# Hash-masked attention and a mixture of experts: new gates and slots for GpSimd's subtractions, other slots for weight copies and scatters, other numbers of idle matmuls

## The chip, the cores and the metric

The kernel runs on one core of a Trainium2 chip. The metric is the time of one execution on the device in microseconds (us). The engines are named as in the profile: PE is TensorE (matmuls; PEld its weight loads), DVE is VectorE, ACT is ScalarE, POOL is GpSimd, SP issues most of attention's DMAs. TensorE's clock has two levels, 1.2 and 2.4 GHz, and the profile gives the granted clock as a share of full speed.

## The reference, cut to what matters

Attention comes first: 4 batches of 8 heads, 768 rows of 64, with a mask of equal hash buckets. Its output, 3072 tokens of 512, goes through a mixture of 8 experts, where a greedy order over all (token, expert) scores assigns at most 384 tokens to each expert.

```
logits = x @ w_gate
flat = logits.flatten()
order = np.argsort(-flat)
assigned = -np.ones(N, dtype=np.int64)
counts = np.zeros(E, dtype=np.int64)
for idx in order:
    tok, e = (int(idx) // E, int(idx) % E)
    if assigned[tok] >= 0 or counts[e] >= cap:
        continue
    assigned[tok] = e
    counts[e] += 1
out = np.zeros((N, D), dtype=np.float32)
for e in range(E):
    mask = assigned == e
    h = np.maximum(x[mask] @ w1[e], 0.0)
    out[mask] = h @ w2[e]
```

N is 3072, D 512, E 8, cap 384, and w1[e] is 512 x 1024.

## The kernel before, in words

The program has two parts in an order written out by hand: each engine runs its instructions as the code lists them. Attention ends near 428 us; the expert part, class Moe, follows, and only that part is touched.

**Phases.** The greedy assignment is done in eight phases. In each phase the expert that fills up first is found ("closed"): DVE takes the best expert left for every token, then a threshold is searched digit by digit in six levels. A level is a comparison on DVE (zcmp), a count on PE (L472 for the first level and all of phase 0, L479 later), a few small DVE steps on the counts (L481 to L563), and a new running value zd (L565, in SBUF, read by the next comparison). After the sixth level come the closing steps: L574 and L575 on PE, L577 to L585 on DVE (L580 makes zwg, L582 asg, L584 and L585 the pair zSTb), then L601 and L602 on PE, which rank the members. Then ohp and Rr on DVE, the collect L611 on PE, and the list of the 384 tokens (zidx). Phase 0 runs alone, between attention and the first expert.

**Blocks and slots.** `Moe.run` lays the experts out in eight blocks of 68 slots (NS). Block k computes the expert of phase k. A slot is a few matmuls: slots 0 to 31 are layer 1 (eight groups f=0 to 7 of four slots, three matmuls each, into two PSUM buffers in turn), slots 32 to 67 layer 2 (three groups c of twelve slots, two matmuls each). Phase k+1 runs inside block k: the lists E1 (phase 1, in block 0), E2 (phase 2) and EV (phases 3 to 6) give the slot at which each step of the phase is put into the order, counted from the start of block k (a negative one lies in the block before it). `XS` and `XS1` give the slots of the next expert's transposes (L709), 57 or 61 and on.

**Both halves of a number.** Weights and activations are split into a rounded part and the rest, and the products of the parts are summed. ACT rounds a quarter of a layer's weights (wh, L691; slots W1 and W11 for layer 1, W2 for layer 2), and POOL subtracts (wl, L701, two instructions per quarter, 16 per expert). After each f ACT writes hh (L737) and DVE writes hl (L738), which frees the PSUM buffer.

**Hands.** The subtractions wait in a list (`s.pend`). `s.hand(n)` puts n of them into POOL's order, behind a copy of one element (ztick, L700) from a tile named by `s.gate`, so that POOL starts only when DVE has written that tile: zd in a level, zsatl after the sixth, zcum and zcc later. HS gives n for each step. A subtraction that no hand took goes out at a slot of its own (L803). On POOL's order stand also the DMAs that gather the tokens (L674), load the next expert's weights (L682) and scatter the outputs (L756, slots by SC).

**Idle matmuls.** `s.warm` puts matmuls of 128 columns on PE that nothing reads (L505). KW holds their numbers for eight places in phase 0 and before the first expert.

Of the kernel before, what the change touches and what calls it, by code (L numbers as in the profile page):

```python
# [8 lines left out]
F32 = mybir.dt.float32  # L9
F32R = mybir.dt.float32r  # L10
F16 = mybir.dt.float16
BF = mybir.dt.bfloat16
I32 = mybir.dt.int32
AF = mybir.ActivationFunctionType
ALU = mybir.AluOpType
# [5 lines left out]
 E0=[3, 5],  # L21
 E1=[3, 4],
 X=[2, 2, 5],
# [12 lines left out]
 OPS='b0 i3 i2 t0 b1 w5 r0 r2 w4 s0 w4 C1 r1 t1 c1 s1 B0 c0 D0 w2 w1 s4 w5 s2 s3 r3 v2 w5 v0 l0 l1 C0 m0 s5 w3 s6 r5 w2 l3 e0 e1 d0 u0 u1 s7 v1 l2 w0 m1 e2 | s8 | x0 | w0 | x1 s9 | r4 s10 | | | s11 m2 v3 f0 | x3 | | x2 | m3 | | | | | |')  # L36
PAT,E0,E1,DW,LEAD=(AP[k] for k in ('PAT','E0','E1','DW','LEAD'))
NB=dict(S=2,T=3,V=1)
HK=385
EMPTY=60000.0  # L40
def attention(tc, nc, ctx, qT, kT, vv, proj, wg, x_dram, L, jp, identf, B, late=None, after=None):
# [183 lines left out]
    def lo(h,kc,eng):  # L225
        p,l=PT[h,kc]
        eng.tensor_tensor(l,p,p.bitcast(BF)[:,1::2],op=ALU.subtract)  # L227
# [93 lines left out]
    def run(n):  # L321
        for f,a in at.get(n,[]): f(*a)
# [5 lines left out]
    for t in range(6*NH+LAG+6):  # L328
        h,s=divmod(t,6)
        first=(t-LAG)%6==5  # L330
        if first: av(t)
        if t<6*NH and t not in early: ST(h,s,0)
        for x in S_at.get(t,[]): S_pass(*x)
        run(2*t)
        if h<NH: ST(h,s,1)
        if t>=1 and (t-1)//6<NH:
            hh,ss=divmod(t-1,6)
            lo(hh,ss,V if ss in (E0 if hh<1 else E1 if hh<2 else PAT[hh%2]) or t==6*NH else G_)
        run(2*t+1)
        if not first: av(t)  # L340
# [5 lines left out]
SH=[25,20,15,10,5,0]  # L346
LOW=[1,1,1,1,1,0]
NT=[128,32,32,32,32,32]
E1=[-12,-4,-3,2,6,7,8,14,20,27,33,36,39,46]
E2=[-9,-8,-6,1,8,15,20,23,27,38]  # L350
EV=[-15,-14,-9,-3,5,12,20,25,29,37]
WL=[4,46]
W1=[45,50,57,63]
W11=[54,55,62,66]
HS=[0,2,2,2,2,2,2,1,1,0]
HB=46
BY=[-1,8,36]
W2=[3,6,10,16]
XS=[57,57,60,63]
XS1=[61,61,64,65]  # L360
KW=[1,0,4,0,2,19,7,1]
SC=15
class Moe:
    def __init__(s, tc, nc, ctx, N):
        s.tc,s.nc,s.N=tc,nc,N
# [67 lines left out]
    def t(s,shape,dt,name,**k): return s.sp.tile(shape,dt,name=name,**k)  # L433
# [73 lines left out]
    def phase(s,ph):  # L507

        nc,NC=s.nc,s.NC; V=nc.vector; T=nc.tensor; G_=nc.gpsimd
        last=ph==7; first=ph==0  # L510
        t=s.z
# [5 lines left out]
        if not last:  # L517
            P=s.Z
            D,E,mxu=P["D"],P["E"],P["mxu"]; d=E[:,0]
            CMP=[P["cmp"][l and 1+l%2] for l in range(6)]  # L520
            if not first:
                for i,f in enumerate(s.best(P,0,NC)):
                    if ph==1 and i==4: yield
                    f()
                s.gate=E[0:1,0,0:1]
                for c0,c1_ in ((0,12),(12,NC)) if ph==1 else ((0,NC),):
                    if ph==1: yield
                    s.compare(CMP[0],0,d,c0,c1_)
            tot=0
            for l,w in enumerate(WID):  # L530
# [3 lines left out]
                if l==0 or first:  # L534
# [3 lines left out]
                    if first:  # L538
                        if l==0: wp=s.wps(); s.warm(KW[7],wp)
                        s.warm(KW[0],wp)  # L540
                    for a,b in ((l+1,l+2),) if first else ((1,6),):
# [9 lines left out]
                if l==0 or first:  # L551
# [4 lines left out]
                    T.matmul(n,s.us[l][0:J],hit[0:J],start=True,stop=True)  # L556
                    if first: s.warm(KW[1],wp)
                else:
# [16 lines left out]
            T.matmul(pe[:,0:8],s.tiny[0:32],sat[0:32],start=False,stop=True)  # L575
            if first: s.warm(KW[2],wp)
            V.reduce_max(nn,pe[:,0:8],axis=AX.X)  # L577
# [23 lines left out]
        T.matmul(pp[:,0:2*NC],s.ntri,STb,start=True,stop=False)  # L601
        T.matmul(pp[:,0:2*NC],s.ones,cum,start=False,stop=True)  # L602
        if first: wp=s.psO.tile([128,512],F32,name="po"); s.warm(KW[3],wp)
        pm=t([128,NC],F32,"pm"); md=t([128,NC],BF,"md"); Gt=t([128,4,NC],F32,"Gt"); junk=t([128,1],F32,"junk")
        mi=t([128,NC],I32,"mi")
        ohp=s.t([128,NC//2,128,2],BF,"ohp",bufs=1); Rr=t([128,2,2,3,NC],BF,"Rr"); acc=t([128,NC],F32,"acc")
        def members(c0,c1):
# [2 lines left out]
        def collect(c0,c1):  # L610
            for g in range(c0,c1): T.matmul(pi[:,0:12],ohp[:,g//2,:,g%2],Rr[:,:,:,:,g],start=g==0,stop=g==NC-1)  # L611
# [2 lines left out]

        V.tensor_scalar(mi,pm.bitcast(I32),0x4583F800,None,op0=ALU.bitwise_and)
        V.tensor_tensor(Gt,pm[:,None,:].to_broadcast([128,4,NC]),s.th,op=ALU.is_ge)
        V.tensor_scalar(md,mi.bitcast(F32),-4096.0,0.0,op0=ALU.add,op1=ALU.add,accum_out=junk)
        def left():

            V.tensor_tensor(A1,wg[:,None,:].to_broadcast([128,8,NC]),s.wt[:,:,None].to_broadcast([128,8,NC]),op=ALU.is_equal)  # L620
            with nc.allow_low_precision("counts up to 24"):
                V.reduce_sum(cc,A1,axis=AX.X)
            s.gate=cc[0:1,0:1]
# [12 lines left out]
        def rr():  # L636
            for i in range(2): V.tensor_tensor(Rr[:,i],Gt[:,None,i:i+3].to_broadcast([128,2,3,NC]),s.gp[:,i,:,None,:].to_broadcast([128,2,3,NC]),op=ALU.mult)
        if first:
            pi=ps()
            for i,b in enumerate(blocks):  # L640
                members(*b)
                if not i: rr()
                collect(*b); s.warm(KW[4],wp)
        else:
# [131 lines left out]
    def run(s):  # L776
        V=s.nc.vector; ch=s.ch; at={}; NS=68
        def add(n,f,*a): at.setdefault(n,[]).append((f,a))
        def end(p):
            s.gather(p)  # L780
            if p<7: next(ch[p+1])
        def step(p,n):
            next(ch[p],None); s.hand(n)
        for p in range(1,8):
            b=NS*(p-1)
            ev=[b+e for e in (E1 if p==1 else E2 if p==2 else EV)]
            dec=ev[-3] if p<7 else ev[-2]-2
            hs=[0]*(len(ev)-10)+HS
            if p==1: hs[3]=2
            if p==7: ev=ev[-2:]; hs=[0,0]  # L790
            for e,n in zip(ev,hs): add(e,step,p,n)
            add(ev[-1],end,p)
            if p>1: add(b-NS+HB,s.hand,2)
            add(max(dec,b+WL[0]),s.wload,p,0); add(max(ev[-1],b+WL[1]),s.wload,p,1)
            for q in range(4):
                add(b+(W11 if p==1 else W1)[q],s.wsplit,p,0,q,None,b+NS+BY[0]+BY[1]*q if p<6 else 0)
                add(b+(XS1 if p==1 else XS)[q],s.xsplit,p,q)
        for k in range(8):
            for q in range(4): add(NS*k+W2[q],s.wsplit,k,1,q,None,NS*k+BY[2] if k<6 else 0)
            for q in range(3): add(NS*k+44+12*q+SC,s.scatter)  # L800
        for n in range(-NS,NS*8):
            for f,a in at.get(n,()): f(*a)
            while s.pend and s.pend[0][0]<=n: s.nc.gpsimd.tensor_tensor(*s.pend.pop(0)[1],op=ALU.subtract)  # L803
            if n<0: continue
            k,h=divmod(n,NS)
            if h<32: s.layer1(k,h//4,h%4)
            else: s.layer2(k,(h-32)//12,(h-32)%12)
        while s.late: s.scatter()
# [52 lines left out]
```

## Time and profile before

| | |
|---|---|
| median of 3 runs | 789.22 us (785.79, 789.22, 791.88) |
| profiled execution | 785.28 us, of which span 783.5 us |
| PE busy | 718.4 us (92%), 7765 matmuls |
| DVE busy | 561.4 us (72%) |
| POOL busy | 550.8 us (70%) |
| ACT busy | 406.0 us (52%) |
| POOL's subtractions L701 | 90, 113.9 us, 1280 ns each |

The span is the time from the first to the last instruction on the core; the rest of the profiled execution's time lies around it. Busy shares are averages over attention and experts, which have different limits. In a row of a timeline stand the start in us, the duration, the engine, the line, the operation, output and inputs, and in brackets how long the engine stood idle before it and what ended that.

### The profile page before, as it was taken

The numbers are of one execution on the slowest core, as the hardware profiler recorded it, in microseconds if no ns is written. First come the engines' busy times: TensorE is split into PE (matmuls) and PEld (weight loads), VectorE is DVE, ScalarE is ACT, GpSimd is POOL, SyncE is SP. The second block draws the span as 40 slices with busy tenths as digits, with TensorE's granted clock in tenths as the row PEclk, the third lists the DMA queues.
The fourth block names the chain that finished last, engine by engine and source line by source line (L and its number), as shares of the span: only waits on it lengthen the run. The fifth ranks groups of instructions, "written<-read, shape, count | busy, mean of one in ns | idle before, by whom it ended". The sixth has DMA issues, their size and how long they took to land. (4 is left out here: it accounts for less than half of the span.)

```text
span 783.5 us, 19133 instructions
## 1 busy us (share of the span) xinstructions
PE 718.4 (92%) x7765; PEld 547.7 (70%) x7765; DVE 561.4 (72%) x1321; ACT 406.0 (52%) x790; POOL 550.8 (70%) x479
## 2 busy tenths in 40 slices
PE   8998999998999998999798579989999999999995
PEld 2566676666666675666566368877888787889894
DVE  5878978778677785988774768888887878753120
ACT  6776686576776766755555042524343334334430
POOL 7696788695785966856565167678878787878761
PEclk9999999999999998999999569999999999999998
DMA  6637734437254272340001160716171717162601
GB/s 182 192 89 194 169 119 126 103 115 167 70 121 109 84 175 51 85 104 22 22 2 41 33 225 1 269 47 236 41 255 41 256 42 255 41 222 92 251 27 41
DMA packets 38320, 92.40 MB, mean 118 GB/s; under 512 B 4452, under 2 KB 28888, under 8 KB 36184
## 3 DMA queue, kind: packets, MB, share of 16 engines
q1 hardware_dynamic: 31416, 45.03, 22.4%
q0 software_dynamic: 6816, 46.15, 16.6%
q8 instruction: 61, 1.00, 0.6%
q14 instruction: 27, 0.22, 0.1%
HBM read 59.53 MB, written 12.58 MB: 92 GB/s over the span
## 5 line engine op out<-in xcount | busy, mean ns | idle before, releaser
L227 POOL TENSOR_TENSOR lo<-pt 128x768 f16<-128x768 f32 x143 | 235.2, 1655 | 102.8 <-ACT pt L224 92.9
L224 ACT ACTIVATE pt<-pst 128x384 f32<-128x384 f32 x384 | 182.9, 491 | 94.0 <-PE pst L223 79.9
L200 DVE TENSOR_REDUCE m<-pss 128x1 f16<-128x770 f32 x192 | 182.6, 956 | 56.4 <-PE pss L198 55.4
L222 PE MATMUL pst<-qa,ka 128*128 128x384 f16 x384 | 128.2, 334 | 9.9 <-ACT pt L224 6.7
L223 PE MATMUL pst<-qb,kb 128*128 128x384 f16 x384 | 127.0, 331 | 0.0
L239 PE MATMUL psv<-vh,lo 128*128 128x65 f16 x1152 | 122.6, 195 | 0.0
L237 PE MATMUL psv<-vh,pt 128*128 128x65 f16 x1152 | 122.6, 196 | 0.0
L238 PE MATMUL psv<-vl,pt 128*128 128x64 f16 x1152 | 122.5, 194 | 0.0
L237 PEld LDWEIGHTS <-pt 128*128 128x128 bf16 x1152 | 107.8, 99 | 13.9 <-issue 4.4
L701 POOL TENSOR_TENSOR wl<-wf,wh 128x512 fp32r<-128x512 f32 x90 | 113.9, 1280 | 0.0
L238 PEld LDWEIGHTS <-pt 128*128 128x128 bf16 x1152 | 106.7, 99 | 10.1 <-issue 0.8
L198 PE MATMUL pss<-ka,qa 96*128 96x385 f16 x384 | 96.9, 334 | 12.9 <-ACT qa L208 7.8
L239 PEld LDWEIGHTS <-lo 128*128 128x128 f16 x1152 | 106.8, 98 | 0.0
L691 ACT CAST wh<-wf 128x1024 fp32r<-128x1024 f32 x64 | 66.4, 1048 | 47.3 <-DMA wf<-in_w_dram,zwidx 47.3
L737 ACT ACTIVATE hh<-ph 128x384 fp32r<-128x384 f32 x64 | 31.4, 491 | 86.7 <-PE ph L735 86.7
L198 PEld LDWEIGHTS <-qa 96*128 96x128 f16 x384 | 37.9, 99 | 45.2 <-issue 23.0
L738 DVE SCALAR_TENSOR_TENSOR hl<-ph,hh 128x384 fp32r<-128x384 f32 x64 | 35.2, 554 | 44.1 <-ACT hh L737 43.6
L735 PE MATMUL ph<-xh,wh 128*128 128x384 f32 x256 | 60.5, 349 | 2.0 <-DVE hl L738 1.2
L227 DVE TENSOR_TENSOR lo<-pt 128x768 f16<-128x768 f32 x49 | 58.6, 1195 | 2.0 <-ACT pt L224 1.9
L735 PE MATMUL ph<-xl,wh 128*128 128x384 f32 x256 | 56.8, 340 | 0.0
L735 PE MATMUL ph<-xh,wl 128*128 128x384 f32 x256 | 56.1, 339 | 0.0
L223 PEld LDWEIGHTS <-kb 128*128 128x128 f16 x384 | 38.2, 99 | 23.7 <-issue 13.5
(258 smaller groups left out, 1399.9 us busy)
## 6 DMA issues: line engine op xcount, KB each, us to landing
vp<-in_vv_dram SPq DMA_DIRECT2D x8, 768.0 KB
x_dram<-X SPq DMA_DIRECT2D x16, 384.0 KB
qp<-in_qT_dram SPq DMA_DIRECT2D x7, 768.0 KB
kp<-in_kT_dram SPq DMA_DIRECT2D x7, 768.0 KB
qa<-qh SPq DMA_DIRECT2D x14, 192.0 KB
ka<-kh SPq DMA_DIRECT2D x14, 192.0 KB
qb<-qh SPq DMA_DIRECT2D x14, 192.0 KB
kb<-kh SPq DMA_DIRECT2D x14, 192.0 KB
```

Of the source, the lines that this page charges most:

```text
L198: T.matmul(ps[:,hf,0:HK],QA[u][0:96,j,qc*128:qc*128+128],KA[u][0:96,j,hf*HK:hf*HK+HK],start=True,stop=True)
L200: V.tensor_reduce(M6[h][:,qc:qc+1],ps[:,:,0:HK],axis=AX.XY,op=ALU.max,negate=True)
L222: T.matmul(ps[:,0:384],KA[u][:,j,kr],QA[u][:,j,r],start=True,stop=False)
L223: T.matmul(ps[:,0:384],KB[u][:,j,kr],QB[u][:,j,r],start=False,stop=True)
L224: A.activation(PT[h,kc][0][:,r],ps[:,0:384],AF.Exp,scale=0.125)
L227: eng.tensor_tensor(l,p,p.bitcast(BF)[:,1::2],op=ALU.subtract)
L237: T.matmul(av[:,c,:],ph[:,r],VH[u][:,j,kc,:],start=(kc==0 and c==0),stop=False,skip_group_check=True)
L238: T.matmul(av[:,c,0:64],ph[:,r],VL[u][:,j,kc,:],start=False,stop=False,skip_group_check=True)
L239: T.matmul(av[:,c,:],l[:,r],VH[u][:,j,kc,:],start=False,stop=False,skip_group_check=True)
L691: s.nc.scalar.copy(h[:,r],f[:,r])
L701: for _ in range(n): s.nc.gpsimd.tensor_tensor(*s.pend.pop(0)[1],op=ALU.subtract)
L735: T.matmul(p[:,0:384],a[:,o:o+128],b[:,d],start=n==0,stop=n==11)
```

## The change

Steps of phase 1 from the count on come three to five slots later in block 0 (E1). HS has other numbers: hands of three behind the first, second, fourth and fifth level's zd, of two behind the third, none behind the sixth level and the closing steps, two behind zcc. The additional hand of two at slot 46 (HB) is gone. The gate at a phase's start is the tile OH, written after E. ACT's rounded weights come at earlier slots: W1 from 45, 50, 57, 63 to 45, 48, 52, 57, and W2 from 3, 6, 10, 16 to 2, 4, 7, 11. Scatters are listed 7 slots after their group's end instead of 15 (SC). KW goes from [1,0,4,0,2,19,7,1] to [1,4,5,10,2,30,5,2]: four idle matmuls more at each level of phase 0 (second number), one and ten more at its closing (third, fourth), eleven more after its list (sixth), two fewer after each of three groups of transposes (seventh), one more at the first count (eighth). The step md no longer writes an accumulator. As two lines fall away, lines of after have numbers one or two lower.

```diff
-E1=[-12,-4,-3,2,6,7,8,14,20,27,33,36,39,46]
+E1=[-12,-4,-3,2,11,12,13,19,25,31,37,40,43,49]
-HS=[0,2,2,2,2,2,2,1,1,0]
-HB=46
+HS=[0,3,3,2,3,3,0,0,2,0]
...
-                s.gate=E[0:1,0,0:1]
+                s.gate=P["OH"][0:1,0,0:1]
...
-        V.tensor_scalar(md,mi.bitcast(F32),-4096.0,0.0,op0=ALU.add,op1=ALU.add,accum_out=junk)
+        V.tensor_scalar(md,mi.bitcast(F32),-4096.0,None,op0=ALU.add)
...
-            if p>1: add(b-NS+HB,s.hand,2)
```

POOL's order in block 3, from the scatter of the block before's last group to the closing of phase 4, before:

```order
L756 DMA out_dram<-o,zidx 3072x512
L700 CAST ztick<-zsatl 1x1
L701 TENSOR_TENSOR wl_10560<-wf_10353,wh_10559 128x512 x2
L700 CAST ztick<-zcum 1x1
L701 TENSOR_TENSOR wl_10560<-wf_10353,wh_10559 128x512
L682 DMA wf_10751<-in_w_dram,zwidx 128x4096
L700 CAST ztick<-zcc 1x1
```

After, from the same scatter:

```order
L755 DMA out_dram<-o,zidx 3072x512
L699 CAST ztick<-zd_10674 1x1
L700 TENSOR_TENSOR wl_10576<-wf_10374,wh_10575 128x512 x3
L681 DMA wf_10765<-in_w_dram,zwidx 128x4096
L699 CAST ztick<-zcc 1x1
L700 TENSOR_TENSOR wl_10576<-wf_10374,wh_10575 128x512 x2
L673 DMA xg<-x_dram,zidx 128x512 x3
```

The hand of two behind zsatl and the one subtraction behind zcum, which stood between the last levels and the load of the next weights, are gone; a hand of three now stands behind the fifth level's zd, after the scatter, and two subtractions instead of one behind zcc, ahead of the gather (xg).

DVE's order at the start of block 0, from the first comparison of phase 1 (zcmp_377), before:

```order
L461 TENSOR_TENSOR zcmp_377<-zE,tb_92 128x1536 x2
L738 SCALAR_TENSOR_TENSOR hl<-ph,hh 128x384
L456 TENSOR_SCALAR zD<-zkey 128x24 x5
L553 TENSOR_SCALAR zsat,zhit<-psa 128x8
L565 SCALAR_TENSOR_TENSOR zd_8898<-zE,psa 128x24
L461 TENSOR_TENSOR zcmp_379<-zd_8898,tb_93 128x768
```

After, from the same comparison:

```order
L460 TENSOR_TENSOR zcmp_377<-zE,tb_92 128x1536 x2
L737 SCALAR_TENSOR_TENSOR hl<-ph,hh 128x384 x2
L455 TENSOR_SCALAR zD<-zkey 128x24 x5
L552 TENSOR_SCALAR zsat,zhit<-psa 128x8
L737 SCALAR_TENSOR_TENSOR hl<-ph,hh 128x384
L564 SCALAR_TENSOR_TENSOR zd_8956<-zE,psa 128x24
L460 TENSOR_TENSOR zcmp_379<-zd_8956,tb_93 128x768
```

The digits (zD), the check of the first count (zsat) and the first level's zd stood behind hl of f=0 alone; now hl of f=0 and f=1 stand ahead of the digits, and hl of f=2 ahead of zd.

## Rows read from the trace of the kernel before

**Rows 1.** Busy time by stretches: start and end, length, then busy time (and count) of PE, PEld, DVE, ACT, POOL, the granted clock, the DMA share and GB/s.

```profile
460.00:480.00 20.00, 16.16 (x114) 14.63 (x113) 16.46 (x61) 8.08 (x17) 12.64 (x13) 0.83 0.30 106
...
550.00:600.00 50.00, 48.55 (x332) 42.90 (x333) 40.36 (x154) 20.42 (x35) 40.19 (x42) 1.00 0.35 124
```

**Rows 2.** The list of PE's waits from 466 to 784 us: what waited for what, us in total, times, longest.

```profile
PE psa L601 <- DVE zwidx L666: 5.4, 4, 2.0
PE psa L601 <- DVE zSTb L585: 1.2, 1, 1.2
```

**Rows 3.** Timelines of POOL, DVE and PE at the closing of phases 4 (block 3) and 2, and L580's durations over the whole run in ns (shortest/median/longest).

```profile
601.43 2.53 POOL L701 TENSOR_TENSOR wl<-wf,wh 128x512 fp32r<-128x512 f32 x2
...
601.90 2.10 DVE L580 SCALAR_TENSOR_TENSOR zwg<-zd,znn,zmxu 128x24 f32<-128x24 bf16 x1
...
L580 DVE SCALAR_TENSOR_TENSOR zwg<-zd,znn,zmxu x7: 232/2042/2098, 444.2 to 681.7; 128x24 f32<-128x24 bf16 x7
...
519.96 3.17 DVE L582 TENSOR_TENSOR asg<-asg,zwg 128x24 f32<-128x24 f32 x1
...
604.72 0.20 PE L601 MATMUL psa<-zSTb,ntri 128*128 128x48 bf16 x1 [1.18 <-DVE zSTb L585]
```

**Rows 4.** Timelines of POOL, DVE and PE in block 3, levels of phase 4.

```profile
584.94 2.54 POOL L701 TENSOR_TENSOR wl<-wf,wh 128x512 fp32r<-128x512 f32 x2
...
588.03 0.24 DVE L565 SCALAR_TENSOR_TENSOR zd<-zd,zn,zE 128x24 bf16<-128x24 bf16 x1
...
588.31 0.56 DVE L461 TENSOR_TENSOR zcmp<-zd,tb 128x768 bf16<-128x768 bf16 x1
...
589.49 0.32 PE L479 MATMUL psa<-zOH,zcmp 128*128 128x32 bf16 x6
...
593.39 0.32 PE L479 MATMUL psa<-zOH,zcmp 128*128 128x32 bf16 x6
```

**Rows 5.** Timelines of PE, POOL, DVE and ACT at the start of block 0.

```profile
458.87 0.96 PE L735 MATMUL ph<-xh,wh 128*128 128x384 f32 x4 [0.28 <-ACT xh L722]
...
461.61 2.49 POOL L701 TENSOR_TENSOR wl<-wf,wh 128x512 fp32r<-128x512 f32 x2
...
461.51 4.27 DVE L461 TENSOR_TENSOR zcmp<-zE,tb 128x1536 bf16<-128x1536 bf16 x2
...
464.97 0.48 PE L472 MATMUL psa<-zOH,zcmp 128*128 128x8 bf16 x12 [2.71 <-DVE zcmp L461]
...
465.50 1.04 ACT L691 CAST wh<-wf 128x1024 fp32r<-128x1024 f32 x1 [4.03 <-DMA wf<-in_w_dram,zwidx]
...
466.97 0.56 DVE L738 SCALAR_TENSOR_TENSOR hl<-ph,hh 128x384 fp32r<-128x384 f32 x1 [1.19 <-ACT hh L737]
...
469.43 1.63 PE L735 MATMUL ph<-xh,wh 128*128 128x384 f32 x4
```

**Rows 6.** Timelines of POOL, PE and DVE in block 0, the third and fourth level of phase 1.

```profile
472.87 0.50 POOL L700 CAST ztick<-zd 1x1 f32<-1x1 bf16 x1 [1.16 <-DVE zd L565]
...
473.57 0.32 PE L479 MATMUL psa<-zOH,zcmp 128*128 128x32 bf16 x6
...
473.93 0.15 DVE L481 TENSOR_TENSOR znt<-rem,psa 32x8 f32<-32x8 f32 x1
...
475.99 0.24 DVE L565 SCALAR_TENSOR_TENSOR zd<-zd,zn,zE 128x24 bf16<-128x24 bf16 x1
...
476.27 0.56 DVE L461 TENSOR_TENSOR zcmp<-zd,tb 128x768 bf16<-128x768 bf16 x1
...
477.47 0.96 PE L735 MATMUL ph<-xh,wh 128*128 128x384 f32 x4 [0.20 <-DVE hl L738]
```

**Rows 7.** Timelines of PE, DVE and POOL at the end of phase 1, and the time from issue to landing of the gathers (xg) over the whole run.

```profile
487.92 0.20 PE L601 MATMUL psa<-zSTb,ntri 128*128 128x48 bf16 x1
...
490.69 0.52 DVE L637 TENSOR_TENSOR zRr<-zGt,gp 128x144 bf16<-128x144 f32 x2
...
491.39 0.81 PE L611 MATMUL psa<-zRr,ohp 128*128 128x12 bf16 x24
...
495.39 1.11 POOL L674 DMA_INDIRECT xg<-x_dram,zidx  x1 [0.30 <-issue]
...
DMA to landing us min/median/max: 3.4/4.3/5.4
...
499.87 0.82 PE L709 MATMUL px<-identf,xg 128*128 128x128 f32 x6
```

**Rows 8.** Phase 0: three stretches (columns as in rows 1), and the timeline of PE for a count of 24 in phase 0 and one in phase 4.

```profile
434.00:436.00 2.00, 1.37 (x27) 1.02 (x27) 1.37 (x9) 0.00 (x0) 0.00 (x0) 0.50 0.01 4
...
454.00:456.00 2.00, 1.82 (x12) 1.76 (x13) 0.99 (x7) 1.15 (x2) 1.66 (x2) 0.50 0.68 184
...
457.00:458.00 1.00, 1.00 (x11) 1.00 (x9) 0.45 (x1) 0.52 (x1) 1.00 (x2) 0.62 0.91 344
...
434.46 0.96 PE L472 MATMUL pst<-zOH,zcmp 128*32 128x8 bf16 x24 [0.60 <-DVE zcmp L461]
...
577.25 0.76 PE L472 MATMUL psa<-zOH,zcmp 128*128 128x8 bf16 x24
```

**Rows 9.** Timelines of ACT and PE at the start of block 6.

```profile
708.06 1.06 ACT L691 CAST wh<-wf 128x1024 fp32r<-128x1024 f32 x1 [2.21 <-DMA wf<-in_w_dram,zwidx]
...
710.15 0.96 PE L735 MATMUL ph<-xh,wh 128*128 128x384 f32 x4 [0.77 <-DVE hl L738]
```

More of the change, by code (lines that the diff above doesn't have):

```diff
@@ L352 @@
 WL=[4,46]
-W1=[45,50,57,63]
+W1=[45,48,52,57]
 W11=[54,55,62,66]
-HS=[0,2,2,2,2,2,2,1,1,0]
-HB=46
+HS=[0,3,3,2,3,3,0,0,2,0]
 BY=[-1,8,36]
-W2=[3,6,10,16]
+W2=[2,4,7,11]
 XS=[57,57,60,63]
 XS1=[61,61,64,65]
-KW=[1,0,4,0,2,19,7,1]
-SC=15
+KW=[1,4,5,10,2,30,5,2]
+SC=7
 class Moe:
@@ L603, in phase @@
         if first: wp=s.psO.tile([128,512],F32,name="po"); s.warm(KW[3],wp)
-        pm=t([128,NC],F32,"pm"); md=t([128,NC],BF,"md"); Gt=t([128,4,NC],F32,"Gt"); junk=t([128,1],F32,"junk")
+        pm=t([128,NC],F32,"pm"); md=t([128,NC],BF,"md"); Gt=t([128,4,NC],F32,"Gt")
         mi=t([128,NC],I32,"mi")
```

## The prediction

> **What bounds the kernel now.** I read the chain of work that ended last first: it holds only the last scatter and its DMA, so the end hangs on TensorE (PE), which feeds the last tiles. The table of stretches comes next [rows 1]: from 550 to 600 us PE is busy 48.6 of 50 us at the full granted clock, from 460 to 480 us only 16.2 of 20 at 0.83. So in the expert part time can only be won where PE stands still or runs at 1.2 GHz. The list of PE's waits [rows 2] names one place: the matmul L601 waits five times, 6.6 us in all, for VectorE's (DVE) closing steps. The timelines say why [rows 3]: the step L580 takes 0.23 us when free and 2.10 us at 601.90, and ends when a pair of GpSimd (POOL) subtractions ends (601.43 + 2.53 = 603.96). At 519.96 L582 takes 3.17 us in the same way. So a DVE step on two SBUF inputs stands until POOL has finished all subtractions that it was handed, not only the running one. One subtraction is 1.27 us.
>
> **Part 1: no hand at the two last steps (HS).** The hands after the sixth level and at the closing are now empty, so L580 and L582 run free there and L601 gets its input about 1.9 us sooner than it did; the wait of 1.18 us at 604.72 [rows 3] and its like, up to 2.0 us [rows 2], should go. The 16 subtractions stay; they move into hands of three behind levels 1, 2, 4 and 5. A hand begins when the compare ends, since POOL's small copy waits for the same step. In blocks 2 to 5 a hand of three from 584.94 [rows 4] would end at 588.74. The level's step L565 (zd), due at 588.03, is held 0.7 us; the compare then ends near 589.4, and its reader on PE stands at 589.49. So the slack is used up and the slip is 0.1 to 0.2 us. The same holds a level later (a hand of two that begins after a scatter, reader at 593.39), and at the next. Behind each compare lies the step hl that frees a PSUM buffer for PE, which slips with it. I take 0.5 us of slip per block against a wait of (6.6 - 2.0) / 4 = 1.15: 0.65 us x 4 = **-2.6 us**, between -4.6 (no slip) and +2 (1.65 us of slip). In block 1, whose slots lie closer (E2), the slips eat all of the 2.0 us: **0**, between -2 and +1.5.
>
> **Part 2: phase 1 at later slots (E1), in block 0.** Before, PE stands 2.71 us at 464.97, because the compare is held by POOL's pair (461.61 to 464.10, compare from 461.51 for 4.27) [rows 5]. After, the count stands five slots later, and the pair waits for OH, a step later than E. That removes this wait, but what is late next stands beside it: ScalarE copies the first quarter of layer 2's weights at 465.50, when its DMA lands, and only then makes hh of f=0; hl of f=0 ends at 466.97 + 0.56 = 467.5. PE has two buffers for layer 1, so f=2 can't start before 467.6, with count or without. A slot of layer 1 is (3.90 - 0.17) / 7 = 0.53 us by the readers at 589.49 and 593.39 [rows 4]; eight slots from 458.87 end at 463.1. PE then idles 4.5 us where it idled 2.71 and worked through the count, the rest of f=1 and the first level. Before, f=2 starts at 469.43, so 1.8 us is won there, and a whole level of phase 1 is owed.
>
> How the level chain runs after: f=2 at half clock (four matmuls 1.63 us at 469.43 [rows 5]) and the count of 24 (0.96 us at half clock [rows 8]) end near 472.5. hh and hl of f=2 now stand ahead of L565 on DVE (0.5 + 0.56), then L565 and the compare: reader of level 1 near 474.6. A level takes 3.4 us undisturbed [rows 6]: reader to first step 0.36 (473.57 to 473.93), to L565 2.06, L565 and compare 0.84 (475.99 to 476.83), and 0.1 to the next reader. Six slots are 3.2 us, so this alone costs 0.2 a level. With a hand of three from the end of the compare (3.8 us), L565 is held 1.3 us: the reader of level 2 comes at 479.2, that of level 3 at 484.8. The latter holds a second price: hl of f=4 stands behind level 2's compare on DVE, and f=6 can't start without its buffer (the row at 477.47 shows that wait, 0.20 us, where one more slot lay between reader and f). Hands of two follow, so levels 4 and 5 come at 488.2 and 491.4, L601 at 494.5. From L601 to the end of Rr are 3.29 us (487.92 to 490.69 + 0.52) [rows 7], so the collect L611 comes at 497.8, against 491.39: 6.4 us later. The third gather is issued 4.0 us after L611 (495.39) and lands 4.3 us later by the median, 506.1; the transposes L709 keep their slot 61, and stood at 499.87. **+6.2 us** at that point, between +2 (the hands hold nothing and only f=2's late start and the buffer wait count) and +8. The new order of ScalarE's copies (W2) has no price of its own here: the copy that waits for the DMA stands before hh of f=0 in both.
>
> At this place a rule speaks for another sum. In the rows a held step waits for the whole hand [rows 3]. The Trainium skill, "SBUF — State Buffer", section "SBUF: two separate sides", says that the shared pair is an exclusive lock held for one whole instruction, and that a GpSimd op or a DVE op on two SBUF inputs blocks the other. By that rule DVE could slip in between two subtractions, and the time would be 789 (the first rival below); the rows at 601.90 and 519.96 disagree with that part.
>
> **Part 3: idle matmuls (KW).** Before the first expert, PE waits for DVE at each level. Four more idle matmuls per level, 0.43 us at half clock (an estimate: 128 columns at 1.2 GHz each), lie in the 0.60 us that the next count waits for its compare: nothing on the path. At the levels PE is busy 1.37 of 2 us and the granted clock is 0.50, that is 1.2 GHz; in 454 to 456 it was busy 1.82 of 2, and the clock rose to 2.4 GHz at 457 to 458 [rows 8]. So with more idle matmuls a rise may come earlier. If it does, a count of 24 takes 0.76 instead of 0.96. I take three levels: **-0.6 us**, between +0.3 (the eleven more after the closing, 1.2 us, reach past the landing of the first gather) and -1.5 (all levels, and the collects). Two fewer idle matmuls after each group of transposes would start PE 0.4 us sooner, but f=2 waits for the DMA anyway: 0.
>
> **Part 4: the rest.** Layer 1's weights are copied at earlier slots and loaded sooner, as the load isn't queued behind a subtraction: in block 6 ScalarE waits 2.21 us for a DMA ahead of hh, and PE 0.77 for it [rows 9]. An earlier load removes that: **-0.8**, between -0.8 and 0. Scatters move forward eight slots on POOL; hands of three stand behind them, 1 us each, and that is in the walk above. The plain subtraction in place of one with an accumulator (md) saves one short read per phase, and no subtraction of POOL runs beside it any more: 0. The dropped hand at slot 46 frees L565 of the first level, where PE had slack. Nothing at the tail changes.
>
> **The sum**, against the profiled execution (785.28 us, span 783.5): -0.6 + 6.2 + 0 - 2.6 - 0.8 = +2.2, so 787.5. The three other runs lie at 785.79, 789.22 and 791.88, and the four average 788.0; I put the same +2.2 on that: **790 us**. One per cent, 7.9 us, is about what a measurement of this kernel tells from no change.
>
> **Rivals.**
> - *DVE slips in between two subtractions.* Then L565 at 477.0 waits only for the second one, which ends there, and part 2 costs 5.0: -1.2, some 789. The two held steps speak against it. This is the rule of the Trainium skill's "SBUF — State Buffer" named above. Chance 0.12.
> - *L601 still waits.* The hand of three behind level 5 begins late, after a scatter, runs to 602.6, and holds L580 (601.90) again. Then part 1 is lost: +2.6, 792.5. Against it: 0.6 us of cover at L601. Chance 0.12.
> - *Faster: block 0 keeps up.* If the later count meets a compare that is ready and the levels aren't held, PE loses neither the 2.71 us at the count nor the waits at L601: -6.6 - 0.8 - 0.6 - 2.7 = -10.7, some 777. For it: these are PE's largest waits. Against it: the landing at 465.5 and the 3.8 us of a hand of three. Chance 0.11.
> - *Slower: the hands of three set the pace in blocks 1 to 5.* Slack between compare and reader is 589.49 - 588.87 = 0.6 us [rows 4]. A hold of 0.7 uses it up; if hands begin 0.6 us later than I put them (a tick takes 0.50 us [rows 6], and it may wait for the compare first), each of three levels in five blocks loses 0.6: +9, and part 1's gain goes: 790 + 9 + 2.6 = 801.6. It decides where the hold passes 0.7. Chance 0.11.
>
> **How the numbers follow.** The forecast, part 2's loss paid back by two thirds by parts 1, 3 and 4, gets 0.54. With the first two rivals, 0.78 lie within 1% of 789.2; 0.11 are faster, 0.11 slower. The range reaches to the near edges of both outer cases, and takes in the bounds of parts 1 to 3 and the spread of the runs: 780 to 798.
>
> **What would show it.** Right: PE waits from 463 to 467.6 for hl; level readers of block 0 stand 4.5 us or more apart; L565 takes up to 1.5 us there and 0.3 to 0.9 in blocks 2 to 5; L580 takes 0.23; L601's wait is gone; blocks 2 to 5 are each some 0.65 us shorter; the first L709 stands near 505.5. Wrong: L565 stays at 0.24 us beside hands of three, f=2 starts before 467, or L601 waits on.

## The result, and the profile of the changed kernel

The changed kernel takes 788.86 us (median of 20 runs, 784.69 to 797.49), the kernel before beside it 784.24 (20 runs, 778.45 to 791.88). The ratio is 1.0059, interval 1.0038 to 1.0081: some 4.6 us slower, 3.0 to 6.4. The forecast of 790 us and "within 1%" came out. The sum behind it did not hold as well: one term that it put at nothing was worth about 4 us, and of the gains set against the loss in block 0 two did not show and one came at most in part.

The profiled execution of the changed kernel took 787.92 us, its span is 785.8. Spans alone don't compare: attention ended 6.6 us sooner in this profile. In all profiles of this study the count of phase 0's second level stands anywhere from 424.2 to 437.7 us, with no code of attention altered. So I read the **expert part**, from that count to the end: 783.5 - 434.46 = 349.0 us before, 785.8 - 427.86 = 357.9 after. It spares the comparison attention's spread, but a single profile of it still differs by up to 5 us from what the ratios say (here +8.9 against +4.6). Part of that is the one profile of before: against it ten of the thirteen later profiles read 0.8 to 4.8 us too slow, and three up to 1.7 too fast. The largest of these gaps is that of the kernel with the old scatter slots, whose profile is the longest of its 11 runs. I trust the part for places, and for sums only where the ratio agrees.

Times of the changed kernel in the first block carry the shift: add 6.6 us to compare them with rows of before. Its lines have numbers 1 lower (L601 is L600), 2 lower at the end.

PE's waits from 459 to 786 us (what waited for what, us in total, times, longest). The waits of L601 [rows 2] are gone; two that were small in the kernel before (1.2 and 0.6 us there, as L735 and L556) stand in their place, L734 for hl and L555 for L552:

```profile
PE ph L734 <- DVE hl L737: 6.7, 8, 3.5
PE psa L555 <- DVE zsat L552: 5.7, 4, 1.5
PE psa L478 <- DVE zcmp L460: 2.5, 3, 1.4
```

Stretches (columns as in rows 1), the first and second 6.6 us earlier than those of [rows 1]; in the third, inside the first, PE has been at half clock throughout:

```profile
453.40:473.40 20.00, 15.75 (x91) 14.04 (x89) 13.11 (x37) 7.44 (x14) 10.87 (x11) 0.66 0.29 105
543.40:593.40 50.00, 48.19 (x332) 41.48 (x331) 40.01 (x152) 21.00 (x38) 39.79 (x39) 1.00 0.39 137
460.00:473.00 13.00, 12.12 (x65) 10.95 (x65) 6.68 (x26) 4.47 (x11) 6.23 (x7) 0.50 0.00 1
```

Block 0, timelines of ACT, PE, DVE and POOL, the answer to [rows 5 to 7]. PE stands 3.53 us for hl (2.71 for the compare before), then the level readers come at 467.17, 473.22, 477.75, 481.14 and 484.46, and L708 at 500.74:

```profile
458.08 1.04 ACT L690 CAST wh<-wf 128x1024 fp32r<-128x1024 f32 x1 [3.48 <-DMA wf<-in_w_dram,zwidx]
460.16 0.69 PE L734 MATMUL ph<-xh,wh 128*128 128x384 f32 x1 [3.53 <-DVE hl L737]
467.11 3.72 POOL L700 TENSOR_TENSOR wl<-wf,wh 128x512 fp32r<-128x512 f32 x3
469.61 1.27 DVE L564 SCALAR_TENSOR_TENSOR zd<-zd,zn,zE 128x24 bf16<-128x24 bf16 x1
473.22 0.32 PE L478 MATMUL psa<-zOH,zcmp 128*128 128x32 bf16 x6
487.83 0.20 PE L600 MATMUL psa<-zSTb,ntri 128*128 128x48 bf16 x1
491.16 0.50 PE L610 MATMUL psa<-zRr,ohp 128*128 128x12 bf16 x13 [0.23 <-DVE zRr L636]
500.74 1.48 PE L708 MATMUL px<-identf,xg 128*128 128x128 f32 x6
```

Blocks 2 to 5: the closing step L579 (durations in ns, whole run) against [rows 3], the level step L564 from 470 to 700 us against the 0.24 us of [rows 4], and the first level of phase 4 at block 3's head, POOL, DVE and PE:

```profile
L579 DVE SCALAR_TENSOR_TENSOR zwg<-zd,znn,zmxu x7: 232/490/528, 437.6 to 685.5; 128x24 f32<-128x24 bf16 x7
...
L564 DVE SCALAR_TENSOR_TENSOR zd<-zd,zn,zE x24: 243/610/1269, 469.6 to 679.9; 128x24 bf16<-128x24 bf16 x24
...
578.98 0.17 PE L472 MATMUL psa<-nrem,moneh 128*128 128x8 f16 x1
579.33 1.00 POOL L755 DMA_INDIRECT out_dram<-o,zidx  x1 [0.30 <-ACT zE L545]
580.99 0.17 DVE L552 TENSOR_SCALAR_CACHE_REDUCE zsat<-psa 128x8 bf16<-128x8 f32 x1 [2.37 <-PE po L746]
581.22 0.16 PE L555 MATMUL psa<-zhit,us 128*128 128x1 bf16 x1 [1.51 <-DVE zsat L552]
```

L579 falls from 2.04 to 0.49 us in the median (0.23 when free), so the closings run nearly as foreseen. But L564 takes 0.61 us where it took 0.24, and at the head of the block L552 starts 1.84 us after the count that it reads has ended (578.98 + 0.17), 0.66 us after the end of a scatter's issue on POOL. In block 3 of the kernel before no scatter stood there.

I call a profile **late** when L552 starts 0.2 us or more after its count at most blocks, and **prompt** when it starts 0.03 to 0.04 us after it wherever DVE is free. The profile of the changed kernel is late, that of the kernel before prompt.

Phase 0 and block 6, against [rows 8, 9]: the counts still take 0.96 us and follow each other after 2.01 us (PE at half clock), and in block 6 ScalarE and PE wait no less than before:

```profile
429.86 0.96 PE L471 MATMUL pst<-zOH,zcmp 128*32 128x8 bf16 x24
431.87 0.97 PE L471 MATMUL pst<-zOH,zcmp 128*32 128x8 bf16 x24
...
710.43 1.05 ACT L690 CAST wh<-wf 128x1024 fp32r<-128x1024 f32 x1 [2.32 <-DMA wf<-in_w_dram,zwidx]
712.52 0.97 PE L734 MATMUL ph<-xh,wh 128*128 128x384 f32 x4 [0.89 <-DVE hl L737]
```

### The profile page after: what moved, and what is told of

It reads as the page before. It is cut to its first block, busy times and chain, and to the rows that moved or that the text cites. A ratio compares the mean times of both kernels' runs of the same rounds, so it can differ in the third digit from the quotient of the medians.

```text
span 785.8 us, 19178 instructions
## 1 busy us (share of the span) xinstructions
PE 722.6 (92%) x7802; PEld 553.0 (70%) x7802; DVE 556.4 (71%) x1313; ACT 404.9 (52%) x790; POOL 548.8 (70%) x464
## 5 line engine op out<-in xcount | busy, mean ns | idle before, releaser
L700 POOL TENSOR_TENSOR wl<-wf,wh 128x512 fp32r<-128x512 f32 x92 | 115.7, 1277 | 0.0
L198 PE MATMUL pss<-ka,qa 96*128 96x385 f16 x384 | 95.3, 329 | 13.1 <-ACT qa L208 8.1
L734 PE MATMUL ph<-xh,wh 128*128 128x384 f32 x256 | 62.9, 360 | 8.1 <-DVE hl L737 6.7
L734 PE MATMUL ph<-xl,wh 128*128 128x384 f32 x256 | 58.0, 345 | 0.0
L734 PE MATMUL ph<-xh,wl 128*128 128x384 f32 x256 | 57.6, 348 | 0.0
L749 ACT COPY o<-po 128x512 f32<-128x512 f32 x24 | 14.1, 587 | 81.8 <-PE po L746 81.8
```

The source lines that it names most:

```text
L198: T.matmul(ps[:,hf,0:HK],QA[u][0:96,j,qc*128:qc*128+128],KA[u][0:96,j,hf*HK:hf*HK+HK],start=True,stop=True)
L700: for _ in range(n): s.nc.gpsimd.tensor_tensor(*s.pend.pop(0)[1],op=ALU.subtract)
L734: T.matmul(p[:,0:384],a[:,o:o+128],b[:,d],start=n==0,stop=n==11)
```

## Experiments

Ratios are to the kernel before, run beside each group: the first four kernels were one group, the next four a second, then three, then one. "Part" is the expert part of the one profile. A steady block is the time from L601 (L600 with the later numbering) of one phase to that of the next, phases 3 to 6. The first and the last group were prompt, the second and the third late.

**Block 0's slots alone.**

```
 before.py
-E1=[-12,-4,-3,2,6,7,8,14,20,27,33,36,39,46]
+E1=[-12,-4,-3,2,11,12,13,19,25,31,37,40,43,49]
```

> The kernel before with one table of the change alone, E1 (the later slots of block 0's digit steps); the computation is whole. The expert part, from the count that opens the second level of phase 0 to the end of the span, takes 349.0 us in the kernel before (783.5 - 434.46) and 357.9 us in the changed one (785.8 - 427.86). Theory: the later slots alone make the loss of block 0, through the hold of 3.5 us in the place of three short ones and the half clock that follows it; block 0's transposes of the next block (L709) then come about 47 to 49 us after the first level of layer 1 instead of 41.0, and the expert part takes 355 to 357 us (ratio to before 1.008). Rival: the loss comes from the idle matmuls and the hands of three that stand beside the new slots; then this kernel keeps within 2 us of 349.

787.01 us, ratio 1.0054 (1.0017 to 1.0091), part 790.6 - 435.50 = 355.1: the theory's value. The transposes L709 come 46.3 us after layer 1's first level, a little short of the 47 to 49 expected. The longest wait of PE is for hl, and L601's stay, as they must:

```profile
PE ph L735 <- DVE hl L738: 6.9, 4, 4.7
PE psa L601 <- DVE zwidx L666: 5.4, 4, 2.0
```

The table costs 6.1 us by the trace and 4.2 by the ratio (1.3 to 7.1), and that without hands of three.

**The change without block 0's slots.**

```
 after.py
-E1=[-12,-4,-3,2,11,12,13,19,25,31,37,40,43,49]
+E1=[-12,-4,-3,2,6,7,8,14,20,27,33,36,39,46]
```

> The changed kernel with the table E1 of the kernel before put back; the computation is whole. Theory (block 0's loss is the table's): block 0 gets back 6 to 7.5 us, the expert part takes 350 to 352 us against 357.9 in the changed kernel, and what is left over 349.0 is the wait of the second level's matmul (L555) for DVE's first result (L552), 1.3 to 1.5 us in each of four blocks, less what the closings gave. Rival (the block loses through the hands of three or the idle matmuls): the expert part stays above 355 us.

776.65 us, ratio 0.9904 (0.9871 to 0.9937), part 345.1, below every expectation; a steady block took 38.7 us. The waits of L555 were gone in blocks 2 to 5, though the table touches only block 0. In block 3 the same instructions stand in the same order at the same distances, and L552 starts at once:

```profile
571.62 0.17 PE L472 MATMUL psa<-nrem,moneh 128*128 128x8 f16 x1
571.83 0.17 DVE L552 TENSOR_SCALAR_CACHE_REDUCE zsat<-psa 128x8 bf16<-128x8 f32 x1 [0.57 <-PE psa L472]
571.97 1.01 POOL L755 DMA_INDIRECT out_dram<-o,zidx  x1 [0.30 <-ACT zE L545]
572.20 0.18 PE L555 MATMUL psa<-zhit,us 128*128 128x1 bf16 x1
```

**The old scatter slots.**

```
 after.py
-SC=7
+SC=15
```

> The changed kernel with the scatters put back to their old slots (SC=15 instead of 7); the computation is whole. In the changed kernel L552 on DVE starts 0.47 to 0.66 us after the end of a scatter's 1.0 us on GpSimd in five blocks of five, though the counts that it reads have ended earlier, and the matmul L555 behind it waits 1.29 to 1.51 us in four of them. Theory (the scatter at slot 51 holds DVE's start there): all these waits go, and the expert part falls from 357.9 to 352 to 354 us. Rival (the scatter stands there by chance, and the start is late for another reason, as in other places where DVE runs through a scatter untouched): the waits of 1.3 to 1.5 us stay, and the expert part stays within 1 us of 357.9.

785.37 us, ratio 1.0009 (0.9991 to 1.0028); part 792.2 - 437.67 = 354.5, just above the theory's 352 to 354, where 357.9 had been. L552 starts promptly in all blocks. I took that as the theory's win, but the kernel above was prompt with its scatters at 7, as the whole group was, so the prompt start decides nothing here.

**Hands and rounding slots alone.**

```
 before.py: HS, W1, W2 as in after.py, and
-            if p>1: add(b-NS+HB,s.hand,2)
```

> The kernel before with the change of the subtractions' hands and of the rounding's slots alone (HS, W1, W2, and no hand at slot 46); the scatters, block 0's slots and the idle matmuls stay as before; the computation is whole. Theory: the closings of blocks 2 to 5 lose the wait of L601 (before 1.97, then 1.31 to 1.43 us), at 0.65 us each, and since the scatters stand where they stood, nothing takes its place at the next block's first level: the expert part takes 345.5 to 347 us against 349.0. Rival: the matmul L556 waits for L553 here too (1.3 to 1.5 us a block), as in the changed kernel, so that it comes from the missing hand and not from the scatter; then the expert part takes 349 to 351 us.

779.46 us, ratio 0.9975 (0.9935 to 1.0014); part 349.9. L601's waits are gone, L556 waited in block 0 alone (0.7 us), and yet a steady block took 39.68 us against 39.86, where 0.65 less was forecast. So neither expectation holds: the theory's part did not come, and the rival's waits did not, though its 349 to 351 did. The gain went to the level step (from 470 to 700 us, here and in before):

```profile
L565 DVE SCALAR_TENSOR_TENSOR zd<-zd,zn,zE x22: 244/646/1748, 471.3 to 667.7; 128x24 bf16<-128x24 bf16 x22
```

```profile
L565 DVE SCALAR_TENSOR_TENSOR zd<-zd,zn,zE x24: 242/244/245, 472.5 to 676.5; 128x24 bf16<-128x24 bf16 x24
```

In a steady block the third and fourth of these steps take 0.73 and 0.64 us, and cost PE little. The fifth takes 1.7: the hand of three that holds it began only behind a scatter (POOL, DVE and PE in block 3).

```profile
584.74 1.37 POOL L756 DMA_INDIRECT out_dram<-o,zidx  x1 [0.17 <-DVE zd L565]
586.26 3.77 POOL L701 TENSOR_TENSOR wl<-wf,wh 128x512 fp32r<-128x512 f32 x3
588.36 1.72 DVE L565 SCALAR_TENSOR_TENSOR zd<-zd,zn,zE 128x24 bf16<-128x24 bf16 x1
590.72 0.32 PE L479 MATMUL psa<-zOH,zcmp 128*128 128x32 bf16 x6 [0.43 <-DVE zcmp L461]
```

The reader waits 0.43 us for it, and PE waits for hl 0.27 us twice a block. In blocks 0 and 1 the hands cost 2.8 us (L601 of block 1 stands 91.95 us after the count, 89.17 before).

**Both tables put back.**

```
 after.py: E1 as in before.py, and
-SC=7
+SC=15
```

> The changed kernel with two tables of the kernel before put back, E1 (block 0's digit steps) and SC (the scatters' slots, 15 instead of 7); the computation is whole. With E1 alone put back the expert part, from the count of phase 0's second level to the end, took 345.1 us and a steady block 38.69 us; with the hands alone in the kernel before (scatters at their old slots) it took 349.9 us and a steady block 39.68 us. Theory: the scatters' earlier slots are what saves the 1.0 us a block, so this kernel's steady blocks take 39.6 to 39.7 us and its expert part 349 to 350 us. Rival: the gain is due to the idle matmuls, the gate of the big compare or the accumulating operation that is gone; then a steady block stays at 38.7 us and the expert part at 345 to 346 us.

780.92 us, ratio 0.9973 (0.9941 to 1.0006), part 778.2 - 430.37 = 347.8, a steady block 39.8 us. The block is the theory's, so the idle matmuls, the gate and the plain md don't make the short block. The part lies 2 us under the theory and 2 over the rival. In three steady blocks L552 started 0.26 to 0.29 us late here, behind the load of the weights (L681), with no scatter near; at 496.46 it stood 1.1 us, behind a scatter.

**Scatters two slots later.**

```
 after.py
-SC=7
+SC=9
```

> The changed kernel with the scatters two slots later (SC=9 instead of 7), so that the first of a block's three is issued at slot 53 with the next block's first digit step, not two slots ahead of it; the computation is whole. In the changed kernel L552 starts 2.69 to 2.85 us after the start of the five digits (L455), behind a scatter of 1.0 us that starts 1.21 us after them, and L555 waits 1.29 to 1.51 us; with E1 put back the same instructions stand in the same order and at the same distances, and L552 starts at 1.07. Theory (the scatter just ahead of L552 is needed for the late start): the waits of L555 go, the steady blocks fall from 40.1 to 40.3 us to 38.7 to 39.7 us, and the expert part falls from 357.9 to 352 to 354 us. Rival (the late start has its cause elsewhere, in what block 0 leaves behind): the waits stay, expert part 357 to 359 us.

787.75 us, ratio 1.0049 (1.0023 to 1.0075), part 354.1. The waits of L555 stay (4.9 us, four times), as the rival says, though its part is 357 to 359. But POOL has nothing to wait for between the gathers and that scatter, so two slots don't put it behind L552: POOL's order is the same, and the run doesn't decide between the two.

**Slots half as late.**

```
 after.py
-E1=[-12,-4,-3,2,11,12,13,19,25,31,37,40,43,49]
+E1=[-12,-4,-3,2,8,9,10,16,22,29,35,38,41,47]
```

> The changed kernel with block 0's digit steps about half as late: 8, 9, 10, 16, 22, 29, 35, 38, 41, 47 in place of 11, 12, 13, 19, 25, 31, 37, 40, 43, 49 (before: 6, 7, 8, 14, 20, 27, 33, 36, 39, 46); the computation is whole. With the old slots the changed kernel's expert part takes 345.1 us, with the new ones 357.9 us, of which 7 us are block 0's (steps to the transposes L708: 65.9 against 72.9 us after the count) and 5.7 us are the waits of L555 in later blocks. Theory A (block 0 pays by the slot, since every digit step ends its chain later, and the later blocks' waits come on top): 3.5 us in block 0 and some or none of the later waits, expert part 348 to 352 us. Theory B (the loss comes at one point, where the gap at half clock begins): all or nothing, 345 to 346 or 357 to 358 us.

788.33 us, ratio 1.0039 (1.0006 to 1.0072), part 352.9. L708 of block 1 comes 69.9 us after the count; with the old slots it is 66.5, with the new 71.9 (the pair below, also late). Block 0 pays by the slot (A), though the part lies 1 us over A's 348 to 352. PE's longest wait for hl was 0.6 us here; L555 waited five times, 8.1 us in all.

**The old idle matmuls.**

```
 after.py: E1 as in before.py, and
-KW=[1,4,5,10,2,30,5,2]
+KW=[1,0,4,0,2,19,7,1]
```

> The changed kernel with two tables of the kernel before put back, E1 (block 0's digit steps) and KW (the numbers of idle matmuls); the computation is whole. With E1 alone put back the expert part took 345.1 us. Theory: the idle matmuls are worth nothing here, because phase 0 stands at 2.01 us a level and at half clock with either number of them: expert part 344.5 to 346 us. Rival: the 30 idle matmuls ahead of the transposes bring block 0 to a higher clock, which this kernel then loses: 346.5 to 349 us.

785.26 us, ratio 1.0025 (0.9995 to 1.0054), part 353.2. As it stood, 8 us would have been the idle matmuls' work. But L552 was late here at every block (5.4 us of waits), and had not been in the kernel with E1 put back. All four kernels of this group were late, those of the first group prompt, whatever their code. So the next group repeated two files unaltered.

**The changed kernel, and the one with E1 put back, once more.**

> The changed kernel once more, unaltered, beside the next kernel. So far L552 started late (0.22 to 1.84 us after its counts, and 0.33 to 0.66 us after the end of GpSimd's last indirect transfer issue ahead of it) at nearly every block of some profiles and at none of others: late in the changed kernel (expert part 357.9 us), with SC=9, with the half-late digits, with the old idle matmuls, and by 0.3 us with SC=15 and the old E1; prompt in the four kernels that were run together first, the one with E1 alone put back among them (345.1 us). Theory A (the state belongs to the place where the group of runs was made, not to the code): this kernel and the next one show it together or not at all; if not, the expert part is 350 to 353 us here. Theory B (it belongs to the code): late again here, expert part 357 to 359 us, and prompt in the next.

> The changed kernel with E1 of the kernel before put back, once more, unaltered; it took 345.1 us for its expert part and 0.990 of the kernel before's time. Theory A (a state of the place of the runs): as prompt or late as the changed kernel beside it; if late, L555 waits 1.1 to 1.7 us in each of four or five blocks, a steady block takes 40.2 us and the expert part 350 to 353 us; if prompt, 345 us again. Theory B (a property of the code): prompt, 345 us, whatever the kernel beside it does. By either, E1 alone costs 5 to 8 us between the two kernels of this pair when both are in one state.

The changed kernel: 789.09 us, ratio 1.0113 (1.0036 to 1.0191; 4 runs), part 786.8 - 430.44 = 356.4. E1 put back: 785.37, ratio 1.0038 (1.0001 to 1.0074), part 779.8 - 428.09 = 351.7. The same file had given 0.9904 before. Both were late, theory A:

```profile
572.22 0.17 DVE L552 TENSOR_SCALAR_CACHE_REDUCE zsat<-psa 128x8 bf16<-128x8 f32 x1 [2.21 <-PE po L746]
572.46 0.16 PE L555 MATMUL psa<-zhit,us 128*128 128x1 bf16 x1 [1.34 <-DVE zsat L552]
```

Within the pair E1 costs 4.7 us by the trace; the ratios differ by 0.0075, but their intervals overlap.

**Scatters behind the first hand.**

```
 after.py: E1 as in before.py, and
-SC=7
+SC=11
```

> The changed kernel with E1 of the kernel before put back and the scatters four slots later (SC=11), so that the first of them stands behind the first digit's tick and hand on GpSimd and can't be issued ahead of L552; the computation is whole. Theory (a scatter ahead of L552 is what the state makes dear): L555 waits at most 0.4 us a block in either state, and the expert part takes 345 to 350 us; in the late state it beats the kernel beside it by 3 to 5 us. Rival (the scatters at slot 51 are what saves 1.0 us a block against slot 59 in the prompt state): a steady block takes 39.7 us as with SC=15, expert part 348 to 350 us in either state.

777.29 us, ratio 0.9906 (0.9867 to 0.9944), part 776.7 - 432.66 = 344.0, in the same late group, 7.7 us under its neighbour: faster than both kernels of the study. The part is below the theory's 345 to 350, and the lead over the neighbour above its 3 to 5. L555 waits 1.1 us in all (4.8 in the neighbour), 0.8 of it at one block, where 0.4 was the most expected. A steady block takes 38.64 us, not the rival's 39.7, and the level step is free again (median 245 ns), since at the fourth level it now falls into a scatter and not into a subtraction. The third still takes 0.73 to 0.75 us, and the fifth starts some 0.46 late, behind a hand of three. The fourth level of one block here (POOL and DVE):

```profile
625.46 2.55 POOL L700 TENSOR_TENSOR wl<-wf,wh 128x512 fp32r<-128x512 f32 x2
628.17 1.02 POOL L755 DMA_INDIRECT out_dram<-o,zidx  x1 [0.17 <-issue]
628.41 0.24 DVE L564 SCALAR_TENSOR_TENSOR zd<-zd,zn,zE 128x24 bf16<-128x24 bf16 x1
```

and in the neighbour:

```profile
584.45 2.54 POOL L700 TENSOR_TENSOR wl<-wf,wh 128x512 fp32r<-128x512 f32 x2
586.34 0.69 DVE L564 SCALAR_TENSOR_TENSOR zd<-zd,zn,zE 128x24 bf16<-128x24 bf16 x1
```

**That number alone.**

```
 before.py
-SC=15
+SC=11
```

> The kernel before with one number altered, the scatters' slots (SC=11 instead of 15); the computation is whole. With the new hands and the old E1, SC=11 gave an expert part of 344.0 us and steady blocks of 38.65 us against 347.8 and 39.8 us at SC=15. Theory (the scatter between two hands of three lets DVE's digit step L564 through, 245 ns instead of 690 in the median; with the old hands of two that step takes 244 ns anyway, and the wait is at L601): the number alone is worth nothing, the expert part stays at 348 to 350 us, L601 still waits 1.1 to 2.0 us a block, ratio 0.998 to 1.002. Rival (the earlier scatter saves 1 us a block by itself, whatever the hands are): 344 to 346 us, ratio 0.990 to 0.995.

780.81 us, ratio 0.998 (0.9942 to 1.0018), part 779.3 - 433.63 = 345.7. The trace is the rival's: a steady block takes 38.75 us against 39.86, and L601's waits fall from 6.6 us [rows 2] to one of 1.3. The ratio's middle is the theory's, its interval reaches the rival's 0.995, so that this number alone is a gain is not shown by the time. The reason for the shorter block stands at the closing of phase 4: the third scatter no longer lies between the last two hands, the last one begins sooner against L580, and holds it for 0.97 us instead of the 2.10 of [rows 3]:

```profile
598.88 0.17 POOL L700 CAST ztick<-zsatl 1x1 f32<-1x1 bf16 x1
599.01 2.53 POOL L701 TENSOR_TENSOR wl<-wf,wh 128x512 fp32r<-128x512 f32 x2
600.62 0.97 DVE L580 SCALAR_TENSOR_TENSOR zwg<-zd,znn,zmxu 128x24 f32<-128x24 bf16 x1
```

## Why the prediction was right, and where it was not

**Block 0's slots (+6.2): right in the sum and the mechanism, single steps by luck.** Alone they cost 6.1 us by the trace and 4.2 by the ratio, 4.7 in the late pair. The walk can be laid on the rows of after, 6.6 us added: f=2 at 466.8 (said 467.6), the levels' readers at 473.8, 479.8, 484.4, 487.7 and 491.1 (474.6, 479.2, 484.8, 488.2, 491.4), L600 at 494.4 (494.5), L610 at 497.8 (497.8), L708 at 507.3 (506.1 in the walk, 505.5 among its signs). The first held L564 took 1.27 us, so its hold was 1.0 and not 1.3. From the first to the second reader 6.0 us passed where 4.6 were said (in the profile's own times the compare was ready at 471.5, and the reader stood at 473.22 behind PE's other work at half clock), from the second to the third 4.5 where 5.6 were said (the hand of three had ended before its step). These two misses cancel, which is luck. What the walk left out is the clock: PE ran at half of it for 13.7 us from 459.5 on, against 6.8 in before, and again for 3.4 us from 500.5 on, behind L555's wait. It didn't make the loss, though: in the second profile of the same file half clock lasted 3.4 us at this place, and L708 came 71.9 us after the count all the same (72.9 here, 65.4 before).

**The hands (-2.6): mechanism right, size not settled.** L579 is nearly free and L601 no longer waits. But alone the hands gave +0.9 us by the trace, -2.0 by the ratio (-5.1 to +1.1): a steady block gained 0.2 us where 0.65 was forecast, and blocks 0 and 1, which the term put at nothing, lost 2.8. That kernel has its scatters at the old slots, and the term was reckoned with the new ones. At the old slots one level of five is held 1.5 us (1.72 less the free 0.24); with the new, in the late profile of after, three are held 0.4 to 0.5 (they take 0.60 to 0.75), no more than the 0.7 of the forecast's working. The rival of the hands of three that set the pace asked for a hold over 0.7: it was met at that one level, with the old scatter slots alone.

**The scatters (0): the step that failed.** "Scatters move forward eight slots on POOL; [...] that is in the walk above." The walk has a scatter ahead of one hand; it prices none at the head of a block, ahead of L552, and no loss or gain from the move. The move does two things. It takes a scatter from ahead of a hand of three: in the prompt group a steady block takes 38.7 us with the new hands and the scatters at 7, and 39.7 with the scatters at 15, whether the rest of the change is there or not. And it puts a scatter ahead of L552: in the late groups L555 then waits 1.3 to 1.5 us a block, and a steady block takes 40.2 us. With the new hands and the old E1, slots 15, 7 and 11 gave parts of 347.8, 351.7 and 344.0 us in two late groups: the move made here costs 3.9 us there, and one half as far gains 3.8 (5.1 and 5.3 by the ratios). At 7 the first scatter stands ahead of L552, at 11 behind the first hand, at 15 between the later ones. The trace of before showed a price in part: a scatter stands right ahead of the hand at 601.43 that holds L580 [rows 3]:

```profile
600.26 1.01 POOL L756 DMA_INDIRECT out_dram<-o,zidx  x1 [0.16 <-issue]
```

So the sum hangs on the group. All its terms but E1's were to give -4.0 us; the changed kernel with the old E1 measured -3.9 by the trace and -7.5 by the ratio in the prompt group, +2.7 and +3.0 in a late one. Both profiles of the changed kernel are late. In a prompt group it would stand near 0.9904 x 1.0054 = 0.996 of before (an estimate from two ratios; not run).

**Idle matmuls (-0.6): no gain shown.** The clock stayed at half through phase 0's levels, with a count every 2.01 us as before, though PE was busy 1.90 of 2 us there (429.4 to 431.4) instead of 1.37 [rows 8]. It rose earlier behind them: half clock ended 19.4 to 21.4 us after the count in the nine profiles with the new numbers, 22.6 to 23.3 in the five with the old, and in the prompt profiles layer 1 began 23.1 and 23.2 us after the count instead of 24.1 to 24.5. Block 0 does not keep that: its transposes come 65.9 us after the count with E1 put back in the prompt group, 65.4 in before. Across two late groups the new numbers give 351.7 against 353.2 us, by the ratios 1.0038 against 1.0025: no sign either way. **Block 6 (-0.8): no gain**, ScalarE waits 2.32 us for its DMA. **Slipping in between two subtractions** did not happen: L565 took up to 1.75 us in the kernel with the hands alone, L564 up to 2.1 with E1 put back, and one subtraction is 1.27. On this the rule of the Trainium skill, "SBUF — State Buffer", section "SBUF: two separate sides", a lock held for one whole instruction, still disagrees with the rows.

From before to the changed kernel the parts of the profiles add up as +0.9 (hands), -2.1 (idle matmuls, gate and md; between a prompt and a late group), +3.9 (scatters), +4.7 (E1) = +7.4 us, against +4.6 by the median and +2.2 forecast. The value of 790 is near 788.86 for a second reason: the forecast stood on the mean of the four runs shown, 788.0, and before's median in 20 runs is 784.24. The sum was 2.4 us too low, its base 3.8 too high; that the two cancel is luck.

## What to carry to other kernels

Where GpSimd both computes and issues DMAs, price the place of each DMA in its queue: moved by a few slots, it shifts every hand behind it, and here that was worth nearly as much as the table that the change seemed to be about. A wait that is taken from one step by moving the work which caused it comes back at the steps that it is moved to, so look for their slack first (0.6 us here; a step of 0.24 us came to take 0.6 to 0.75, and 1.7 where the hand that held it began behind a scatter). When two kernels differ by one per cent, run the same file twice in different groups before explaining the difference.

## What the runs showed of the hardware

**A late signal from PE that belongs to the group of runs.** L552 reads PSUM and waits for PE alone. In the late groups it started up to 1.84 us after its counts, often 0.31 to 0.66 us after POOL had issued its last indirect DMA; in the prompt ones it started 0.03 to 0.04 us after them wherever DVE was free, four times in the midst of such an issue. The same file was 0.990 of before in one group and 1.004 in another. It isn't DVE that is held: in the profile of after L455 runs through a gather, and L562, the same kind of instruction on SBUF, through a scatter at 514.66. What comes late is the signal of PE. In the trace the semaphore that L552 waits for rises at 580.97 in after, 1.82 us past the count's modelled end; in the first profile with E1 put back it rises 0.02 us past it. ScalarE's copies of the transposed tokens (L721) wait for PE too, and show the same, late in after and at once with E1 put back:

```profile
448.95 0.75 PE L720 MATMUL px<-identf,xg 128*128 128x128 f32 x4
450.58 1.07 ACT L721 CAST xh<-px 128x512 fp32r<-128x512 f32 x2 [2.64 <-PE psa L720]
```

```profile
449.18 0.66 PE L720 MATMUL px<-identf,xg 128*128 128x128 f32 x4 [0.65 <-DMA xg<-x_dram,zidx]
449.87 1.31 ACT L721 CAST xh<-px 128x512 fp32r<-128x512 f32 x2 [0.87 <-PE px L720]
```

Whether PE's work or only its report is late is not told, since the profile models the ends of matmuls. That a scatter ahead of L552 makes a late group dear is shown: in one such group L555 waits 4.8 us with the scatters at 7 and 1.1 at 11. What sets the late signal off is open: each group ran on another chip, and a chip, a core or something left from earlier would all fit.

**A DMA issue on POOL lets DVE's two-input steps through; a subtraction doesn't.** L564 took 0.24 us inside a scatter's issue, and 0.60 to 2.1 beside hands of two and three. Of 64 such steps in all profiles (level and closing steps) that began inside an issue 62 were free. The other two, L582 at 519.96 in before [rows 3] and at 526.86 in the kernel with block 0's new slots alone (3.15 us), stood until the hand behind the issue had ended.
